# A linear attention with an MLP on one core: the second head of each pair without its swapped copy of v

## The chip, the cores and the metric

One core of a Trainium2 chip runs the whole program. The metric is the time of one execution in device microseconds (us); lower is better. TensorE (PE) multiplies matrices into PSUM, VectorE (DVE), ScalarE (ACT) and GpSimd (POOL) work element by element, and DMA transfers are issued from the queues of SyncE (SP) and of ScalarE.

## What is computed

Four batches of 768 tokens, eight heads of 48 columns. For each head a 48 x 48 state is carried over the tokens, and what it reads out is the x of an MLP with a gate over the tokens:

```python
for t in range(S):
    cur = einsum('bhd,bhe->bhde', u * k_t, v_t)
    y[t] = einsum('bhd,bhde->bhe', r_t, state + cur)
    state = w[:, None] * state + einsum('bhd,bhe->bhde', k_t, v_t)
x = y                                  # (4, 768, 384), heads side by side
u = x + (x^T @ U @ V)^T                # rank 32, over the tokens
out = u + relu(u @ w_ch1) @ w_ch2      # 384 -> 1536 -> 384
```

## The kernel before

**Chunks.** Each batch is six chunks of 128 tokens, and each chunk two halves (i = 0, 1) of 64. The names carry the chunk's number n, from 0 to 23. Within a half, r and k are scaled by powers of w (the tables tabT and tab), so that token-by-token decay becomes a product of matrices: scores = k r^T, masked to earlier tokens (am), times v, plus r times the state at the half's start. The states of successive halves are S; SW is S times w to the power of a half.

**Places on the partitions.** The heads go in pairs q, with j = 0 or 1 in a pair. After a transpose by TensorE (a_tr), head j of a pair has its columns on partitions 64 j to 64 j + 47 of rT and kT. p_sc makes the scores of a half i for head j with the input on half j of the partitions; it writes them to half i for j = 0 and to the *other* half for j = 1 (i ^ j). p_su makes what a half adds to the state. p_out multiplies am with v and rT with S into two PSUM banks pav, one for each row (0, 1: the half of the partitions that is read). Since the scores of j = 1 stand on the other half's partitions, v of the odd heads is loaded a second time with its halves exchanged, as vsw (a_load_odd, two DMAs a chunk). All fp32 products that read one half of the partitions and write one half stand in one of four quarters of the array.

**The steps of a chunk.** a_ks scales k by tab (ks); a_tr transposes r and k and scales them out of PSUM (k by wi, a power of w for each column); a_dv makes r k u, a_dg sums it and multiplies v with the sums, head by head (dv, the token's own term); a_visit(n) is one step of TensorE: the scores and state products of chunk n + 1 first, then the outputs of chunk n; a_am masks the scores, a_st adds up the states and scales them, a_x adds pav of row 0 and of row 1 to dv, which gives x.

**Stages.** The first batch (front(n), n < 6) is worked on alone; filler products ("wake") keep TensorE busy there. Its x goes through c_gx (sums into Gs), then c_xu makes u in two parts (uTh, uTl) and the hidden layer starts: m_1 multiplies u with the first weights, m_2 adds the second product to the output; both weights are loaded and split by VectorE and ScalarE beside it. The chunks of the batches 1 to 3 (18 visits) stand between the products of the MLP of the batch before.

**What sets the order.** Every step is recorded with a due time and a duration in a table of costs, and a planner (class Plan) lays out the order of each engine once, when the program is built. A step that several engines can do goes to the one that the planner expects to be done first. Each engine then runs its order strictly, so a step that waits holds those behind it on its engine.

## Time and profile before

| what | value |
|---|---|
| time, median of 3 runs | 417.44 us (417.15 to 418.97) |
| the profiled execution | 418.57 us, its span 416.9 us |
| PE busy | 401.8 us, 96% |
| DVE busy | 285.4 us, 68% |
| ACT busy | 178.7 us, 43% |
| POOL busy | 63.7 us, 15% |
| DMA | 47.09 MB, 199521 packets |
| granted clock | 0.998 |

The page's busy shares are means over stages of different kinds. The first 50 us are the first batch; up to about 150 us the weights are converted and batch 1 is worked on beside the MLP of batch 0; from there to 340 us follow batches 2 and 3, and then the rest of the last MLP. In the timeline a row has its start, its length, the engine, the line, the operation, output and inputs, and in brackets how long the engine was idle before it and what released it.

### The profile page before, as it was taken

To read this page: it belongs to the slowest core of one execution; us is meant where nothing else is said; L and a number is where in the kernel's file an instruction comes from. 1 tells how busy PE (TensorE), PEld (TensorE's weight loads), DVE (VectorE), ACT (ScalarE), POOL (GpSimd) and SP (SyncE) were. 2 spreads that over 40 slices of the span, in tenths; PEclk is the share of its full clock that TensorE was granted. 3 is DMA by queue.
4 is the path that set the end of the run, shared out by engine and by line. 5 is a ranking of instruction groups with operands and counts; after the bars stand their busy time and mean duration, and the time that the engine had idled before them with its cause. 6 is when DMAs were issued, how large, how long until landed. Compare 5 with 4: busy or idle time off the path is not lost.

```text
span 416.9 us, 12303 instructions
## 1 busy us (share of the span) xinstructions
PE 401.8 (96%) x5112; PEld 387.0 (93%) x5112; DVE 285.4 (68%) x642; ACT 178.7 (43%) x445; POOL 63.7 (15%) x106
## 2 busy tenths in 40 slices
PE   7798899999999999999999999999999999999994
PEld 7798799989999999999999999999999999999994
DVE  7788898899999997787939759788523462113112
ACT  1578478585644464222124433222424442232330
POOL 1462300044240542103000011110000000000000
PEclk9999999999999999999999999999999999999999
DMA  9987879786976777598458765853100420001001
GB/s 136 149 166 199 205 147 216 188 200 126 247 158 105 170 127 173 76 184 163 96 86 162 116 152 80 155 98 76 60 2 2 79 93 0 2 0 60 0 2 62
DMA packets 199521, 47.09 MB, mean 113 GB/s; under 512 B 183073, under 2 KB 197922, under 8 KB 199458
## 3 DMA queue, kind: packets, MB, share of 16 engines
q1 hardware_dynamic: 194274, 44.75, 53.3%
q10 hardware_dynamic: 5184, 1.48, 2.1%
q8 instruction: 42, 0.69, 0.7%
q14 instruction: 21, 0.17, 0.1%
HBM read 37.95 MB, written 8.26 MB: 111 GB/s over the span
## 4 chain that ended last, share of the span: by engine, by line
PE 70%; DVE 12%; DMA 8%; SPq 4%; ACT 3%; issue 2%; ACTq 1%; DVEq 0%
PE p L344 58%; DMA raw_w<-in_moe_w_ch_dram 4%; PE pab L776 2%; SPq L678 2%; PE pav L814 2%; DMA vsw<-in_v_dram 2%; PE pav L820 2%; PE pab L791 2%; DMA ldv<-in_v_dram 2%; DVE raw_w L546 1%; DVE raw_w L543 1%; DVE hl L1108 1%; DVE x L888 1%; PE wake L344 1%; SPq L515 1%
## 5 line engine op out<-in xcount | busy, mean ns | idle before, releaser
L344 PE MATMUL p<-uTh,w1s 128*128 128x384 f32 x576 | 148.1, 338 | 0.2 <-ACT hr L1106 0.2
L1108 DVE TENSOR_TENSOR hl<-hr,hh 128x384 fp32r<-128x384 f32 x90 | 50.7, 564 | 103.9 <-ACT hh L1107 102.4
L1106 ACT ACTIVATE hr<-p 128x384 f32<-128x384 f32 x96 | 47.0, 490 | 169.1 <-PE p L344 164.6
L344 PE MATMUL p<-w2s,hh 128*128 128x384 f32 x576 | 118.9, 338 | 0.0
L344 PEld LDWEIGHTS p<-uTh,w1s 128*128 128x128 f32 x576 | 103.0, 188 | 1.9 <-ACT hr L1106 1.2
L344 PEld LDWEIGHTS p<-w2s,hh 128*128 128x128 f32 x576 | 100.6, 188 | 1.2 <-DVE x L1146 0.3
L344 PE MATMUL p<-uTl,w1s 128*128 128x384 f32 x288 | 96.4, 335 | 0.0
L344 PE MATMUL p<-w2s,hl 128*128 128x384 f32 x288 | 66.4, 335 | 0.5 <-DVE hl L1108 0.5
L344 PEld LDWEIGHTS p<-uTl,w1s 128*128 128x128 f32 x288 | 54.1, 188 | 0.0
L344 PEld LDWEIGHTS p<-w2s,hl 128*128 128x128 f32 x288 | 51.3, 188 | 0.8 <-DVE hl L1108 0.8
L1107 ACT CAST hh<-hr 128x384 fp32r<-128x384 f32 x96 | 49.2, 512 | 2.6
L708 ACT ACTIVATE dv<-ldv,dg 128x48 f32<-128x48 f32 x88 | 21.3, 325 | 4.7 <-DVE dg L704 4.7
L776 PEld LDWEIGHTS pab<-rT,kT 48*64 48x64 f32 x768 | 13.6, 134 | 8.1 <-issue 3.7
L776 PE MATMUL pab<-rT,kT 48*64 48x64 f32 x768 | 17.0, 224 | 2.6 <-DVE rT L747 1.4
L1146 DVE TENSOR_TENSOR x<-p,x 128x384 f32<-128x384 f32 x33 | 16.3, 545 | 3.1 <-PE p L344 3.1
L688 POOL MEMSET ks<- 128x128 f32 x24 | 4.9, 206 | 88.2 <-PE pab L791 86.2
L344 PE MATMUL wake<-ident 128*128 128x128 f32 x114 | 16.4, 299 | 1.7 <-POOL ident masks.py:199 1.7
L881 DVE TENSOR_TENSOR am<-pab,mask 128x256 f32<-128x256 f32 x48 | 17.9, 412 | 0.0
L814 PE MATMUL pav<-vsw,am 64*64 64x48 f32 x384 | 17.1, 220 | 0.1
L814 PE MATMUL pav<-ldv,am 64*64 64x48 f32 x384 | 17.1, 220 | 0.0
L344 PEld LDWEIGHTS wake<-ident 128*128 128x128 f32 x114 | 15.4, 215 | 1.7 <-POOL ident masks.py:199 1.7
L918 POOL TENSOR_TENSOR SW<-S,wm 112x192 f32<-112x192 f32 x24 | 12.2, 508 | 29.0 <-DVE S L909 27.5
(134 smaller groups left out, 506.0 us busy)
## 6 DMA issues: line engine op xcount, KB each, us to landing
raw_w<-in_moe_w_ch_dram SPq DMA_DIRECT2D x24, 384.0 KB, 5.3
ldv<-in_v_dram SPq DMA_DIRECT2D x24, 192.0 KB, 4.3
out_dram<-x SPq DMA_DIRECT2D x21, 192.0 KB, 2.1
ldr<-in_r_dram SPq DMA_DIRECT2D x20, 192.0 KB, 3.8
ldk<-in_k_dram SPq DMA_DIRECT2D x20, 192.0 KB, 3.6
bl<-in_r_dram SPq DMA_DIRECT2D x79, 48.0 KB, 2.5
bl<-in_k_dram SPq DMA_DIRECT2D x79, 48.0 KB, 2.7
ud<-x SPq DMA_DIRECT2D x18, 192.0 KB, 3.1
```

What stands on the lines that cost most here:

```text
L344: return nc.tensor.matmul(*args, **kw)
L678: dma(lambda eng, g=g, s0=s0, ln=ln, sv=sv: eng.dma_start(t.t[32 * g:32 * g + 32, q, :, s0:s0 + ln], sv), [(t, (q, g, s0))], [], 384, 128, ...
L708: nc.scalar.activation(dv.t[:, h], vt()[:, h], AF.Copy, scale=dg.t[:, h:h + 1])
L776: return [lambda q=q, i=i: nc.tensor.matmul(pt.t[(i ^ j) * C2:(i ^ j) * C2 + C2, q * C2:(q + 1) * C2], lhsT=kT.t[rows, q, i * C2:(i + 1) * ...
L791: return nc.tensor.matmul(pt.t[j * HP:j * HP + m, SU + q * D:SU + (q + 1) * D], lhsT=ks.t[half, 2 * q + j, :m], rhs=vt()[half, 2 * q + j, ...
L814: return nc.tensor.matmul(to(q, j, i), lhsT=am[j].t[half, q, :], rhs=vsw[n].t[half, q, :] if j else vt()[half, 2 * q, :], start=(q == 0), ...
L881: on_dve(256, lambda e: e.tensor_tensor(am.t, abs_[n][j].t[:, :SU].rearrange("p (h t) -> p h t", h=NP), mask_.unsqueeze(1).broadcast_to([1 ...
L918: e.tensor_mul(dec.t, new.t, wm.t.broadcast_to([PD, NP, D]))
L1106: on_act(384, lambda: nc.scalar.activation(hr.t, pt.t[:, :TB], AF.Relu), [hr], [pt])
L1107: on_act(384, lambda: nc.scalar.copy(hh.t, hr.t), [hh], [hr])
L1108: on_either(384, lambda e: e.tensor_tensor(hl.t, hr.t, f32(hh.t), ALU.subtract), [hl], [hr, hh])
L1146: on_dve(384, lambda e, x=x, pt=pt: e.tensor_tensor(x.t, pt.t[:, :DM], x.t, ALU.add), [x], [pt])
```

## The change

The scores of j = 1 now stay on their own half (p_sc), so that both heads of a pair take the same v, and vsw with its DMAs is gone. In p_out the 8 value products of a row then read and write that row's half; the state products of that row are four on the same half (together "own", 12) and four on the other ("far"), in the order own, far, own, own. They now take the decayed state SW in place of S, since k's scaling by wi is left out of kT, which becomes a plain copy; tab changes accordingly (its table tw is a copy). Where there is no state yet, the far products take a matrix of zeros (none).

In the first batch alone, a visit becomes two steps (scores and states of chunk n + 1; outputs of chunk n), dv is added by TensorE with the identity (p_dv), a_x is a copy by ScalarE of row 1 and one addition by VectorE, and k from the third chunk on is scaled by GpSimd. In the other batches the two additions of a_x become one step. The copy of tab goes from ScalarE to VectorE. In the planner's table a product of c_gx counts 115 and not 225, the gate products of m_2 now depend on hh, and S and SW have 2 and 4 buffers for 4 and 2.

```diff
...
@@ -451,18 +449,16 @@
         on_dve(4, lambda e: e.tensor_mul(wm.t, top(0), top(0)), [wm], [sq])
 
         tw = xbuf([PD, NP, C], F32, "bl", 5, "tw")
-        on_dve(512, lambda e: e.tensor_mul(subs(tw.t), table(1), wm.t.unsqueeze(2).broadcast_to([PD, NP, 2, C2])), [tw],
-               [wm, tabT], port=True)
+        on_dve(512, lambda e: e.tensor_copy(subs(tw.t), table(1)), [tw], [tabT], port=True)
         on_dve(128, lambda e: e.tensor_mul(tt[:, 0, :, :HC], pw[:, 0], top(1).broadcast_to([PD, NP, HC])), [tabT], [sq])
-        on_dve(4, lambda e: e.tensor_mul(wi.t, top(1), top(1)), [wi], [sq])
         pt = bank("tr", "pt_tab")
 
...
         pe(900, turn, [pt], [tw])
-        on_act(384, lambda: nc.scalar.copy(tab.t.rearrange("p (h d) -> p h d", d=D),
-                                           pt.t.rearrange("p (h d) -> p h d", d=HP)[:, :, :D]), [tab], [pt])
+        on_dve(384, lambda e: e.tensor_copy(tab.t.rearrange("p (h d) -> p h d", d=D),
+                                            pt.t.rearrange("p (h d) -> p h d", d=HP)[:, :, :D]), [tab], [pt])
 
     def flags():
 
...
@@ -645,19 +641,6 @@
             dma(lambda q, i=i, src=src: q.dma_start(part(i)[:, :, :D], src[b, :, c * C:(c + 1) * C, :].rearrange("h p d -> p h d")),
                 [ts[i]] if n < 4 else [(ts[i], "d")], [], 1024, 192, eng=eng)
         rs[n], ks_[n], vs[n] = [((lambda i=i: part(i)), (([(t3, i), (t3, f"pad{i}")] if i < 2 else [tv]) if n < 4 else [(ts[i], "d"), (ts[i], f"pad{i}")])) for i in range(3)]
-        if n < 4 or not front(n):
-            a_load_odd(n)
-
-    def a_load_odd(n, dk=0.0):
-
-        b, c = divmod(n, NCH)
-        t = (xbuf([128, NP, D], F32, "x", NX, f"vsw_{n}") if front(n) else wbuf([128, NP, D], F32, "vsw", 3, f"vsw_{n}"))
-        for i in range(2):
-            s0 = c * C + i * C2
-            dma(lambda q, i=i, s0=s0: q.dma_start(t.t[(1 - i) * C2:(2 - i) * C2],
-                                                  v[b, 1::2, s0:s0 + C2, :].rearrange("h p d -> p h d")),
-                [(t, i)], [], 256, 192, ns=610, eng="ACT" if n < 3 else "SP", dk=dk)
-        vsw[n] = t
 
     bls = {}
 
@@ -687,7 +670,7 @@
         ks = kss[n] = wbuf([128, H, HP], F32, "ks", NK, f"ks_{n}")
         op("POOL", 250, lambda: nc.gpsimd.memset(ks.t[:, :, D:], 0.0), [(ks, "pad")], [])
         on_either(384, lambda e: e.tensor_mul(ks.t[:, :, :D], kt()[:, :, :D], by_head(tab.t)), [(ks, "d")], kb + [tab],
-                  only="DVE" if front(n) else None)
+                  only=("POOL" if n > 1 else "DVE") if front(n) else None)
 
     def a_dv(n):
         (rt, rb), (kt, kb) = rs[n], ks_[n]
@@ -746,18 +729,9 @@
         if i == 0 or n == 0:
             on_dve(512, lambda e: e.tensor_tensor(subs(xT.t[:PD]), subs(by_pair()), table(i), ALU.mult), [xT], [pt, tabT])
             return
-
-
-        def four(q0=0, q1=NP):
-            for q in range(q0, q1):
-                nc.scalar.activation(xT.t[:PD, q], by_pair()[:, q], AF.Copy, scale=wi.t[:, q])
-        if front(n) and n > 1:
-            for q in range(0, NP, 2):
-                op("ACT", 2 * act(C) - 94, lambda q=q: four(q, q + 2), [(xT, q)], [pt, wi])
-            return
-        one_of([("ACT", NP * (act(C) - 94) + 94, four, False),
-                ("DVE", dve(512), lambda: nc.vector.tensor_mul(xT.t[:PD], by_pair(), wi.t.broadcast_to([PD, NP, C])), False)],
-               [xT], [pt, wi])
+        one_of([("ACT", act(512), lambda: nc.scalar.copy(xT.t[:PD], by_pair()), False)]
+               + ([] if front(n) else [("DVE", dve(512), lambda: nc.vector.tensor_copy(xT.t[:PD], by_pair()), False)]),
+               [xT], [pt])
 
 
 
@@ -773,8 +747,8 @@
         rT, kT = trs[n]
         pt = abs_[n][j]
         rows = head_rows(j)
-        return [lambda q=q, i=i: nc.tensor.matmul(
-            pt.t[(i ^ j) * C2:(i ^ j) * C2 + C2, q * C2:(q + 1) * C2], lhsT=kT.t[rows, q, i * C2:(i + 1) * C2],
+        return [lambda q=q, i=i ^ j: nc.tensor.matmul(
+            pt.t[i * C2:(i + 1) * C2, q * C2:(q + 1) * C2], lhsT=kT.t[rows, q, i * C2:(i + 1) * C2],
             rhs=rT.t[rows, q, i * C2:(i + 1) * C2], start=True, stop=True) for q in range(NP) for i in range(2)]
 
     def p_su(n, i):
...
@@ -804,29 +779,38 @@
         vt = vs[n][0]
         rT = trs[n][0]
         pt = pav[row]
+        half = slice(row * C2, (row + 1) * C2)
+        rows = head_rows(row)
+
+        def to(h, i):
+            return pt.t[i * C2:(i + 1) * C2, h * D:(h + 1) * D]
+
+        def av(h):
+            return nc.tensor.matmul(to(h, row), lhsT=am[h % 2].t[half, h // 2, :], rhs=vt()[half, h, :],
+                                    start=(h == 0), stop=False, skip_group_check=True)
+
+        def sq(q, i):
+            rhs = decayed[n, i].t[rows, q, :] if (n, i) in decayed else none.t[rows, :]
+            return nc.tensor.matmul(to(2 * q + row, i), lhsT=rT.t[rows, q, i * C2:(i + 1) * C2], rhs=rhs,
+                                    start=(i != row and q == 0), stop=False, skip_group_check=True)
+
+        def by_state(i):
+            if (n, i) not in decayed and (n == 0 or i == row):
+                return []
+            return [lambda q=q: sq(q, i) for q in range(NP)]
+        own, far = [lambda h=h: av(h) for h in range(H)] + by_state(row), by_state(1 - row)
         ps_ = []
-
-        def to(q, j, i):
-            return pt.t[i * C2:(i + 1) * C2, (2 * q + j) * D:(2 * q + j + 1) * D]
-
-        def av(q, j, i):
-            half = slice(row * C2, (row + 1) * C2)
-            return nc.tensor.matmul(to(q, j, i), lhsT=am[j].t[half, q, :],
-                                    rhs=vsw[n].t[half, q, :] if j else vt()[half, 2 * q, :],
-                                    start=(q == 0), stop=False, skip_group_check=True)
-
-        def sq(q, i):
-            rows = head_rows(row)
-            return nc.tensor.matmul(to(q, row, i), lhsT=rT.t[rows, q, i * C2:(i + 1) * C2], rhs=St[n, i].t[rows, q, :],
-                                    start=False, stop=(q == NP - 1), skip_group_check=True)
-        for q in range(NP):
-            for i in range(2):
-                ps_.append(lambda q=q, i=i: av(q, i ^ row, i))
-        for q in range(NP):
-            for i in range(2):
-                if (n, i) in St:
-                    ps_.append(lambda q=q, i=i: sq(q, i))
+        while own or far:
+            ps_ += own[:1] + far[:1] + own[1:3]
+            own, far = own[3:], far[1:]
         return ps_
+
+    def p_dv(n, row):
+
+        half = slice(row * C2, (row + 1) * C2)
+        return [lambda: nc.tensor.matmul(pav[row].t[half, :DM], lhsT=ident_[half, half],
+                                         rhs=dvs[n].t[half].rearrange("p h d -> p (h d)"), start=False, stop=True,
+                                         skip_group_check=True)]
 
     def in_turn(*lists):
         for k_ in range(max(map(len, lists))):
...
@@ -871,9 +855,16 @@
         def visit():
             in_turn(*other)
             in_turn(*mine)
-        pe(1750 if nxt else 900, visit, wr, rd, tiled=True)
-        if nxt:
-            taken(n + 1)
+        if front(n):
+            if nxt:
+                pe(850, lambda: in_turn(*other), abs_[n + 1], reads(n + 1), tiled=True)
+                taken(n + 1)
+            own = [*ams[n], *vs[n][1], trs[n][0]] + [decayed[n, i] for i in range(2) if (n, i) in decayed]
+            pe(1150, lambda: [in_turn(*mine), in_turn(p_dv(n, 0), p_dv(n, 1))], list(pav), own + [dvs[n]], tiled=True)
+        else:
+            pe(1750 if nxt else 900, visit, wr, rd, tiled=True)
+            if nxt:
+                taken(n + 1)
         a_x(n)
 
     def a_am(n, j):
@@ -884,9 +875,15 @@
     def a_x(n):
         dv = dvs[n]
         x = xs[n] = xbuf([128, DM], F32, "x", NX, f"x_{n}")
-        for row, more in ((0, lambda: dv.t.rearrange("p h d -> p (h d)")), (1, lambda: x.t)):
-            on_dve(384, lambda e, row=row, more=more: e.tensor_tensor(x.t, pav[row].t[:, :DM], more(), ALU.add),
-                   [x], [pav[row], dv])
+
+        def both():
+            nc.vector.tensor_tensor(x.t, pav[0].t[:, :DM], dv.t.rearrange("p h d -> p (h d)"), ALU.add)
+            nc.vector.tensor_tensor(x.t, pav[1].t[:, :DM], x.t, ALU.add)
+        if front(n):
+            on_act(384, lambda: nc.scalar.copy(x.t, pav[1].t[:, :DM]), [x], [pav[1]])
+            on_dve(384, lambda e: e.tensor_tensor(x.t, pav[0].t[:, :DM], x.t, ALU.add), [x], [pav[0]])
+        else:
+            op("DVE", 2 * dve(DM) - 76, both, [x], [*pav, dv])
 
     held = {}
 
...
@@ -910,9 +907,7 @@
                        [new], [pt, decayed[n, j]])
             nk = (n, 1) if j == 0 else (n + 1, 0)
             St[nk] = new
-            if nk[0] % NCH == NCH - 1 and nk[1] or nk[0] % NCH == 0 and nk[1] == 0:
-                continue
-            dec = decayed[nk] = wbuf([PD, NP, D], F32, "SW", 2, f"SW_{nk[0]}_{nk[1]}")
+            dec = decayed[nk] = wbuf([PD, NP, D], F32, "SW", 4, f"SW_{nk[0]}_{nk[1]}")
 
             def one(e, dec=dec, new=new):
                 e.tensor_mul(dec.t, new.t, wm.t.broadcast_to([PD, NP, D]))
...
@@ -1130,7 +1125,7 @@
         if gates:
             for i in range(TPB):
                 pt = ops[b * NCH + t * TPB + i]
-                pe(MM, lambda i=i, pt=pt: gate(i, pt), [pt], [Gs[b], V3])
+                pe(MM, lambda i=i, pt=pt: gate(i, pt), [pt], [Gs[b], V3, hh])
         parts = [(part, m, h, i) for part, m, h in ((high, 2, hh), (low, 1, hl)) for i in range(TPB)]
         if b == B - 1 and t == NTB - 1 and last:
 
...
```

What that makes of the orders is seen in three places.

TensorE's outputs of chunk 13 (the second of batch 2), the rows that follow its next scores. Before:

```order
L814 MATMUL pav0_86<-ldv_13_2566,am_13_0_3012 64x48
L814 MATMUL pav1_98<-vsw_13_2576,am_13_1_3023 64x48
L814 MATMUL pav0_86<-vsw_13_2576,am_13_1_3023 64x48
L814 MATMUL pav1_98<-ldv_13_2566,am_13_0_3012 64x48
L814 MATMUL pav0_86<-ldv_13_2566,am_13_0_3012 64x48
```

And after:

```order
L789 MATMUL pav0_95<-ldv_13_2511,am_13_0_2965 64x48
L789 MATMUL pav1_102<-ldv_13_2511,am_13_0_2965 64x48
L794 MATMUL pav0_95<-SW_13_1_2968,rT_13_2503 64x48
L794 MATMUL pav1_102<-SW_13_0_2834,rT_13_2503 64x48
L789 MATMUL pav0_95<-ldv_13_2511,am_13_1_2975 64x48
L789 MATMUL pav1_102<-ldv_13_2511,am_13_1_2975 64x48
L789 MATMUL pav0_95<-ldv_13_2511,am_13_0_2965 64x48
L789 MATMUL pav1_102<-ldv_13_2511,am_13_0_2965 64x48
```

pav0 is row 0 and pav1 row 1. Before, a row's products alternate between the two halves that they write; after, one in four of them (on SW of the other half) writes the other half.

ScalarE's queue at the start of the program. Before:

```order
L657 DMA vsw_0_91<-in_v_dram 64x4x48 x2
L385 ACT_TABLE_LOAD
L385 COPY outside_76<-ident_67 1x1
L645 DMA ld_0_105<-in_k_dram 128x8x48
L1275 COPY sel_120<-ident_67 128x384
L645 DMA ld_1_109<-in_k_dram 128x8x48
L657 DMA vsw_1_137<-in_v_dram 64x4x48 x2
L645 DMA ld_2_114<-in_k_dram 128x8x48
L657 DMA vsw_2_184<-in_v_dram 64x4x48 x2
L464 COPY tab_206<-pt_tab_195 128x384
```

And after:

```order
L384 ACT_TABLE_LOAD
L384 COPY outside_76<-ident_67 1x1
L1271 COPY sel_91<-ident_67 128x384
L641 DMA ld_0_106<-in_k_dram 128x8x48
L641 DMA ld_1_111<-in_k_dram 128x8x48
L641 DMA ld_2_115<-in_k_dram 128x8x48
L691 ACTIVATE dv_0_171<-ldv_0_127,dg_0_243 128x48 x4
L732 COPY kT_1_274<-ptk_1_247 112x512
```

Three loads of k are all that is left of the DMAs there; the copy of tab is on VectorE, behind rT of chunk 0.

TensorE where the hidden layer starts. Before:

```order
L344 MATMUL wake2_1043<-V3_941 128x512 x4
L344 MATMUL p2_0_0_1072<-Gs_0_1035,V3_941 128x384
L344 MATMUL p2_1_0_1076<-Gs_0_1035,V3_941 128x384
L344 MATMUL p2_2_0_1081<-Gs_0_1035,V3_941 128x384
L344 MATMUL p1_0_0_0_1085<-uTh_0_0_1054,w1s_0_933 128x384 x2
```

And after:

```order
L343 MATMUL wake2_1006<-V3_900 128x512 x4
L343 MATMUL p1_0_0_0_1036<-uTh_0_0_1017,w1s_0_894 128x384 x2
L343 MATMUL p1_0_0_0_1036<-uTl_0_0_1028,w1s_0_894 128x384
L343 MATMUL p1_0_0_0_1036<-uTh_0_0_1017,w1s_0_894 128x384 x2
L343 MATMUL p1_0_0_0_1036<-uTl_0_0_1028,w1s_0_894 128x384
```

p1 are the products of m_1, p2 those of m_2 with the gate products on Gs. Before, the three gate products stand ahead of the first p1; after, they stand behind the second group of p1.

More of the change, by code (lines that the diff above doesn't have):

```diff
@@ L604, in rwkv_moe @@
     NB = B * NCH
-    rs, ks_, vs, vsw = {}, {}, {}, {}
+    rs, ks_, vs = {}, {}, {}
     kss, dvs, dgs = {}, {}, {}
@@ L799, in rwkv_moe @@
     pav = [Buf(ps, [128, 512], F32, None, 1, f"pav{row}") for row in range(2)]
+    none = cbuf([PD, D], F32, "none")
     def p_out(n, row):
@@ L861, in a_visit @@
         nxt = (n + 1) % NCH
-        rd = [*ams[n], vsw[n], *vs[n][1], trs[n][0]] + [St[n, i] for i in range(2) if (n, i) in St]
+        rd = [*ams[n], *vs[n][1], trs[n][0]] + [decayed[n, i] for i in range(2) if (n, i) in decayed]
         wr = list(pav)
@@ L900, in a_st @@
                 continue
-            new = wbuf([PD, NP, D], F32, "S", 4, f"S_{n}_{j}")
+            new = wbuf([PD, NP, D], F32, "S", 2, f"S_{n}_{j}")
             pt = abs_[n][j]
@@ L1269, in rwkv_moe @@
     SOON = 3
+    at(-101, lambda: on_dve(48, lambda e: e.memset(none.t, 0.0), [none], []))
     for p in pav:
```

8 lines of the change are left out of this document (2 added, 6 removed).

## The prediction

> **What bounds the kernel now.** I read the page's busy tenths first (TensorE at 9 from 50 us to the end), then the windows, then the chain of waits from its end backwards.
>
> ```profile
> 40.00:50.00 10.00, 8.32 (x184) 7.51 (x181) 8.96 (x19) 4.13 (x9) 3.47 (x6) 1.00 0.88 216
> 50.00:150.00 100.00, 98.12 (x1254) 91.92 (x1255) 95.37 (x211) 64.25 (x164) 25.45 (x31) 1.00 0.81 171
> ```
>
> The columns of a window are PE, weight load, DVE, ACT and POOL busy time, then the granted clock and the DMA share. From 50 us on TensorE hardly pauses (98.12 of 100), at a granted clock of 1.00. Before 50 us it idles or runs filler, while VectorE is at 8.96 of 10. So two things set the end: when the first hidden-layer products start, and how much work TensorE has after that. The chain of waits in the second half shows that work; its columns are start, length, what:
>
> ```profile
> 153.94 0.62 PE pab L776 x32
> 154.56 0.45 PE pab L791 x27
> ...
> 163.56 0.40 PE pav L820 x14
> ...
> 195.15 0.62 PE pab L776 x32
> ...
> 196.70 0.47 PE pav L820 x30
> 197.16 8.01 PE p L344 x45
> ...
> 216.73 0.61 PE pav L814 x32
> 217.34 0.47 PE pav L820 x32
> ```
>
> Between the p rows stand the visits: scores (L776) and state products (L791) of the next chunk, then the value (L814) and state (L820) products of this one. Each visit delays p by its whole length: 195.15 to 197.16 is 2.01 us, and a chunk's outputs alone, 216.73 to 217.81, are 1.08.
>
> **Part 1, the visits.** A product here works in one quarter of the array, given by the half of the partitions it reads and the half it writes. Each of these fp32 products stands as two records. In the kernel before, the 16 value and 16 state products of a visit (row by row, i by i) put 8 into each quarter, so 16 records. Two comparisons tell what the time goes by. First, scores and states alone put 16 records into the fullest quarter and take 1.08 (153.94 to 155.02), the outputs alone 16 and 1.08, a full visit 32 and 2.01. So 16 further records in a quarter cost 2.01 - 1.08 = 0.93, or 58 ns each. Second, the batch's first visit has state products for the second half only: 16 records in two quarters, eight each. They take 0.40 (14 of the 16 in that row) where 32 records in four quarters, also eight each, take 0.47. Half the work, nearly the same time: the fullest quarter sets it.
>
> After the change the scores stay on their own half, so all 8 value products of an output row read and write the same half: one quarter takes 8 value and 4 state products (24 records), its neighbour 4 (8 records). The fullest quarter gets 8 records more, 8 x 58 ns = 0.465 us per visit. A visit without an earlier state, or without next scores, also goes from 16 to 24 output records in its fullest quarter. There are 18 visits in batches 1 to 3, all where TensorE is full: 18 x 0.465 = **+8.4 us**. Below, the bound is 0 (if something else than the quarter sets it, the first rival); above, 16.7, if the neighbour's products also have to wait their turn in the written order (16 products in a row instead of 8). I take 8.4, because both comparisons give the fullest quarter. The small zero products for chunks without a state go into the emptier quarter: 0.
>
> **Part 2, the start of the first batch.**
>
> ```profile
> 7.55 0.56 DVE L696 TENSOR_TENSOR dv<-ld 128x384 f32<-128x384 f32 x1 [0.60 <-DMA ld<-in_k_dram]
> 9.24 3.17 ACTq L657 DMA_DIRECT2D vsw<-in_v_dram  x2
> 9.83 0.68 DVE L747 TENSOR_TENSOR rT<-ptr,tabT 112x512 f32<-112x512 f32 x1
> 12.45 0.48 ACT L464 COPY tab<-pt_tab 128x384 f32<-128x384 f32 x1 [8.05 <-DMA vsw<-in_v_dram]
> 12.96 1.03 DVE L689 TENSOR_TENSOR ks<-ld,tab 128x384 f32<-128x384 f32 x2 [1.99 <-ACT tab L464]
> 12.98 0.69 PE L776 MATMUL pab<-rT,kT 48*64 48x64 f32 x32 [1.18 <-ACT tab L464]
> ```
>
> The copy of the table sits on ScalarE's queue behind the loads of the swapped v. Those are gone and the copy goes to VectorE, right behind rT: 9.83 + 0.68 + 0.55 = 11.06, and the first k scaling follows there instead of at 12.96: -1.9. The load of the first k was also issued behind two swapped loads, and VectorE waited 0.60 for it: up to -0.6 more. I take **-2.2**; bounds -1.0 (another load late) and -2.5.
>
> **Part 3, the middle chunks of the first batch.**
>
> ```profile
> 22.93 0.69 PE L776 MATMUL pab<-rT,kT 48*64 48x64 f32 x32
> 32.74 0.69 PE L776 MATMUL pab<-rT,kT 48*64 48x64 f32 x32
> L881 DVE TENSOR_TENSOR am<-pab,mask 128x256 f32<-128x256 f32 x12 | 4.6, 415 | 0.0
> L909 DVE TENSOR_TENSOR S<-pab,SW 112x192 f32<-112x192 f32 x10 | 3.5, 351 | 1.7 <-PE pab L791 1.2 <-ACT SW L922 0.5
> L918 DVE TENSOR_TENSOR SW<-S,wm 112x192 f32<-112x192 f32 x3 | 1.4, 459 | 0.0
> L689 DVE TENSOR_TENSOR ks<-ld,tab 128x384 f32<-128x384 f32 x4 | 2.3, 585 | 2.0 <-ACT tab L464 2.0
> L759 DVE TENSOR_TENSOR kT<-ptk,wi 112x512 f32<-112x512 f32 x1 | 0.7, 678 | 0.0
> L708 ACT ACTIVATE dv<-ldv,dg 128x48 f32<-128x48 f32 x48 | 11.8, 328 | 4.2 <-DVE dg L704 4.2
> 41.44 1.57 PE L344 MATMUL pv<-raw_v,sel 128*96 128x192 f32 x8 [0.17 <-DMA ldv<-in_v_dram]
> ```
>
> Two chunks took 9.81, so 4.9 each. After, a chunk's outputs are a step of their own behind its scores, and the next scores stand behind them in TensorE's order. The loop is then: scores and states 1.08; S 0.35, am 0.41, SW 0.46, am 0.41 on VectorE, since the state products now read the decayed state (SW); outputs 1.08 + 0.465; and the new sum of dv by TensorE. That last is two 384-column fp32 products side by side, which no row shows. The nearest, pv, takes 1.57 for eight records of 192 columns, 0.20 each: a record of twice the columns would take 0.40, two of them 0.8 (upper bound); at p's pitch (8.01 / 45 = 0.18 for 384 columns) two take 0.36 (lower). I take 0.6, the middle. Sum 1.08 + 1.63 + 1.55 + 0.6 = 4.9, as now: **0**, with bounds of 0.2 a turn either way. What leaves the engines there (an x addition of 0.55 (42.09 below) per chunk and the later k scalings of 0.585 off VectorE, one kT copy for four activations on ScalarE) lies beside this loop. The added wait is that TensorE now stands for dv, made by eight activations of 0.328 on ScalarE; behind it wait the next scores. Eight of them, 2.6, and two copies of about 0.5 fit into a turn of 4.9.
>
> GpSimd now scales k, four times. Its price is a collision:
>
> ```profile
> 42.09 0.55 DVE L888 TENSOR_TENSOR x<-pav,dv 128x384 f32<-128x384 f32 x1
> 44.13 1.03 POOL L696 TENSOR_TENSOR dv<-ldr,ldk 128x384 f32<-128x384 f32 x1
> 44.64 0.94 DVE L546 SCALAR_TENSOR_TENSOR raw_w<-raw_w 128x384 int32<-128x384 int32 x1
> 45.50 0.55 DVE L543 SCALAR_TENSOR_TENSOR raw_w<-raw_w 128x384 int32<-128x384 int32 x1
> ```
>
> While GpSimd multiplied, a weight step on VectorE took 0.94 against 0.55. Four more GpSimd steps: between 0 and 4 x 1.03; I take one such collision, **+0.4**. The Trainium skill ("SBUF — State Buffer", the single rule on the shared port pair) says that a VectorE instruction with two SBUF inputs and a GpSimd one that reads SBUF exclude each other for a whole instruction; by that, the cost would be near the upper end, and this one row shows a delay of 0.39.
>
> **Part 4, the end of the first batch.**
>
> ```profile
> 37.38 1.91 PE L344 MATMUL wake<-x,Uf 128*96 128x128 f32 x16 [1.09 <-issue]
> 49.23 0.55 DVE L954 TENSOR_TENSOR Gs<-wake,Gs 32x384 fp32r<-32x384 f32 x1
> 52.29 1.37 PE L344 MATMUL p<-Gs,V 96*128 96x384 f32 x3
> 53.50 0.51 PE L344 MATMUL p<-uTh,w1s 128*128 128x384 f32 x2
> ```
>
> Today it is 16.5 from the fifth chunk's scores (32.74) to the end of the sums (Gs, 49.23). After: one turn 4.9, last scores 0.85, pv 1.57 and seven x sums 1.7 (two records each, 0.12 a record, by the row at 37.38), outputs and dv 2.15, eight x sums 1.9, nine transposes 1.1, three x sums 0.7, the two copies into Gs 0.75 (an estimate: the 0.55 of the row at 49.23 and the start of a shorter one before it): 15.6, so **-0.9**, bounds +1.0 and -3.0. Then three gate products stand ahead of the first hidden-layer products and hold TensorE from 52.29 to 53.50, though three need 3 x 0.18 = 0.53; they now come after the first two groups, when nothing holds them: 1.21 - 0.53, some **-0.8** with the first group's earlier start (0 to -1.2).
>
> **Part 5, weights.**
>
> ```profile
> 71.56 0.36 DVE L536 TENSOR_SCALAR raw_w<-raw_w 128x384 int32<-128x384 uint8 x1 [1.57 <-DMA raw_w<-in_moe_w_ch_dram]
> 72.44 0.62 PE L344 MATMUL p<-w2s,hl 128*128 128x384 f32 x2 [0.49 <-DVE hl L1108]
> ```
>
> VectorE waited 1.57 for a weight from SP's queue, the step behind (hl) came late, and TensorE stood for it at 72.44. Twelve swapped loads that SP issues before that weight are gone, at a time when its queue is one issue behind the other: this wait goes, **-0.6** (0 to -1.5).
>
> **Sum**: 8.4 - 2.2 + 0 + 0.4 - 0.9 - 0.8 - 0.6 = +4.3. The profiled execution took 418.57 (span 416.9 and 1.7 around it), so 422.9; it lies 1.1 above the median of 417.44, so **421.7** is what I predict for the median.
>
> **Rivals.** (1) *The half, not the quarter.* If products that read the same half wait for each other, a visit has 16 output products per half before and after, and costs nothing more: 421.7 - 8.4 = **413.3**. For it: nothing but that all full visits are balanced by half too. Against it: the 0.40 row, which should then be near 0.24. The Trainium skill ("TensorE: Matmul & The Clock Gate", Part 3, the mechanism) states that a weight load overlaps running products only where the row group differs, which is this rival; the row of 0.40 disagrees.
> (2) *The first batch is bound by VectorE's sum.* Then it shortens by what leaves VectorE: six additions 3.3, four scalings 2.3, a kT 0.7 and the idle 2.0, less four more SW 1.8 and the table 0.55, so 6.0 instead of 2.7 (parts 2 to 4 without the gates); 8.4 - 6.0 - 0.8 - 0.6 = +1.0: **418.4**, no change. For it: VectorE is 8.96 of 10 busy, and 95.37 of 100 up to 150 us. Against: the loop of part 3, and TensorE's 98.12 beside that.
> (3) *The split costs.* The transposes of a chunk on TensorE (eight of 0.13 by the row below, 1.0 a chunk) now lie between scores and outputs, and dv may come late; if they aren't covered by the 1.63 of VectorE, four turns grow by 1.0 each: **425.7**.
>
> ```profile
> 43.50 1.04 PE L344 MATMUL pu<-ident,x 128*128 128x128 f32 x8
> ```
>
> That the swapped copy's loads are hidden anyway would take away parts 2 and 5 (to 424.5), inside the range.
>
> **Numbers.** Forecast 0.51 (own range 419 to 424), (1) 0.10, (2) 0.25, (3) 0.14. Leaving out (1) and about half of (3): 416.5 to 426.0. A change of less than 0.5%, 2.1 us, can't be told from none: faster is below 415.4, nearly only (1), 0.12; within, 0.29, most of (2) and the low tail of the forecast; slower 0.59.
>
> **What would show it.** Full visits in the second half of 2.47 instead of 2.01 and outputs alone of 1.55 prove part 1; 2.01 makes (1) right. The first scores near 10.8, the table on VectorE behind rT; the fifth chunk's scores near 30.5; Gs near 46.5, the first p<-uTh near 50; no wait near 69 to 72. A first p<-uTh before 46 makes (2) right, one after 53 (3). I am wrong in the total if visits don't lengthen, or if the first batch gains more than twice what I say.

## The result, and the profile after

| | before | after |
|---|---|---|
| median of four runs each, us | 417.41 | 424.20 (423.65 to 425.2) |
| ratio | | 1.0157, 95% interval 1.0126 to 1.0189 |
| profiled execution, us | 418.57 | 425.20 |
| its span, us | 416.9 | 423.3 |
| first scores of the first batch | 12.98 | 11.00 |
| scores of its second, third, fourth, fifth, last chunk | 17.44, 22.93, 27.75, 32.74, 39.21 | 15.15, 21.71, 26.63, 32.64, 38.23 |
| Gs on VectorE | 49.23 | 49.24 |
| first products with the second weights (w2s) | 57.60 | 57.35 |
| first scores of the third batch | 153.94 | 154.57 |

The change made the kernel slower by 6.8 us. First the visits, in the chain of waits of the changed kernel (start, length, what):

```profile
197.09 0.62 PE pab L750 x32
...
199.55 8.01 PE p L343 x45
...
219.59 0.19 PE pav L789 x2
...
221.12 8.01 PE p L343 x45
```

A full visit now delays p from 197.09 to 199.55, by 2.46 (2.01 before), and outputs alone take 219.59 to 221.12, 1.53 (1.08 before). That is 0.45 for each of 18 visits, 8.1 in all. So everything else together gained only 1.3 (8.1 - 6.8). Where it did not gain is seen in the first batch; this is TensorE's timeline there, with the idle time before an instruction and what ended it in brackets:

```profile
11.00 0.69 PE L750 MATMUL pab<-rT,kT 48*64 48x64 f32 x32
15.15 0.69 PE L750 MATMUL pab<-rT,kT 48*64 48x64 f32 x32 [0.34 <-DVE rT L730]
21.71 0.33 PE L750 MATMUL pab<-rT,kT 48*64 48x64 f32 x4
26.63 0.33 PE L750 MATMUL pab<-rT,kT 48*64 48x64 f32 x4
31.90 0.25 PE L789 MATMUL pav<-ldv,am 64*64 64x48 f32 x1 [0.39 <-issue]
32.64 0.33 PE L750 MATMUL pab<-rT,kT 48*64 48x64 f32 x4
37.13 0.26 PE L789 MATMUL pav<-ldv,am 64*64 64x48 f32 x2 [0.81 <-issue]
49.85 0.50 PE L343 MATMUL wake<-V 96*128 96x512 f32 x1 [0.49 <-DVE Gs L949]
52.30 0.59 PE L343 MATMUL p<-uTh,w1s 128*128 128x384 f32 x2
54.63 0.55 PE L343 MATMUL pu<-ident,x 128*128 128x128 f32 x3 [0.52 <-DVE uTl L1032]
```

The first scores come 1.98 earlier than before. Three turns later, at the fifth chunk's scores (32.64), the lead is 0.10: from the second chunk's scores to there it takes 17.49 instead of 15.30. Gs is not earlier at all. Two of TensorE's pauses are ended by "issue": the engine waited for nothing that the profile shows. The windows after answer those quoted of before:

```profile
40.00:50.00 10.00, 9.51 (x128) 8.46 (x128) 7.73 (x15) 5.48 (x13) 4.28 (x7) 1.00 0.45 75
50.00:150.00 100.00, 98.32 (x1258) 93.79 (x1259) 95.67 (x210) 65.47 (x165) 27.44 (x30) 1.00 0.76 161
```

VectorE is freer than before from 40 to 50 us (7.73 of 10 instead of 8.96) and not from there to 150 (95.67 of 100).

### The profile page after: what moved, and what is told of

It is laid out like the page before. It is cut to its first block, busy times and chain, and to the rows that moved or that the text cites. A ratio compares the mean times of both kernels' runs of the same rounds, so it can differ in the third digit from the quotient of the medians.

```text
span 423.3 us, 12252 instructions
## 1 busy us (share of the span) xinstructions
PE 411.5 (97%) x5130; PEld 396.4 (94%) x5130; DVE 283.8 (67%) x635; ACT 182.2 (43%) x448; POOL 70.0 (17%) x105
## 3 DMA queue, kind: packets, MB, share of 16 engines
q10 hardware_dynamic: 3552, 1.18, 1.1%
## 4 chain that ended last, share of the span: by engine, by line
PE 93%; DVE 4%; ACT 1%; issue 1%; POOL 0%; DVEq 0%; POOLq 0%
PE p L343 71%; PE pav L789 5%; PE pav L794 4%; PE pab L750 3%; PE wake L343 3%; PE pab L765 2%; PE ptk L721 1%; PE pav L811 1%; PE ptr L721 1%; PE pu L343 1%; PE pG L959 1%; DVE x L1141 1%; DVE uTl L1032 0%; ACT dv L691 0%; PE ph L343 0%
## 5 line engine op out<-in xcount | busy, mean ns | idle before, releaser
L1103 DVE TENSOR_TENSOR hl<-hr,hh 128x384 fp32r<-128x384 f32 x91 | 52.4, 575 | 104.9 <-ACT hh L1102 99.3
L794 PE MATMUL pav<-SW,rT 48*64 48x48 f32 x704 | 37.3, 226 | 0.0
L789 PE MATMUL pav<-ldv,am 64*64 64x48 f32 x768 | 28.6, 219 | 1.2 <-issue 1.2
L789 PEld LDWEIGHTS pav<-ldv,am 64*64 64x64 f32 x768 | 25.8, 134 | 3.1 <-issue 2.1
L794 PEld LDWEIGHTS pav<-SW,rT 48*64 48x64 f32 x704 | 28.6, 132 | 0.0
L750 PEld LDWEIGHTS pab<-rT,kT 48*64 48x64 f32 x768 | 14.8, 134 | 6.1 <-issue 5.1
L750 PE MATMUL pab<-rT,kT 48*64 48x64 f32 x768 | 17.9, 224 | 0.3 <-DVE rT L730 0.3
L906 DVE TENSOR_TENSOR S<-pab,SW 112x192 f32<-112x192 f32 x40 | 13.9, 347 | 5.7 <-PE pab L765 5.7
```

The source lines that it names most:

```text
L750: return [lambda q=q, i=i ^ j: nc.tensor.matmul(pt.t[i * C2:(i + 1) * C2, q * C2:(q + 1) * C2], lhsT=kT.t[rows, q, i * C2:(i + 1) * C2], r ...
L789: return nc.tensor.matmul(to(h, row), lhsT=am[h % 2].t[half, h // 2, :], rhs=vt()[half, h, :], start=(h == 0), stop=False, skip_group_chec ...
L794: return nc.tensor.matmul(to(2 * q + row, i), lhsT=rT.t[rows, q, i * C2:(i + 1) * C2], rhs=rhs, start=(i != row and q == 0), stop=False, s ...
L906: on_dve(192, lambda e, new=new, ptv=ptv, dec=decayed[n, j]: e.tensor_tensor(new.t, ptv(), dec.t, ALU.add), [new], [pt, decayed[n, j]])
L1103: on_either(384, lambda e: e.tensor_tensor(hl.t, hr.t, f32(hh.t), ALU.subtract), [hl], [hr, hh])
```

## The experiments

Three groups of kernels ran. Where a text says "the changed kernel's 424.2", that is the median above; the kernel before had medians of 417.78, 417.27 and 417.31 beside the three groups.

### Is it the fullest quarter?

**Swapped copy back in batches 1 to 3** (the first batch stays as changed):

```
-  lambda q, i=i ^ j: matmul(pt[i*C2:(i+1)*C2, ...], kT, rT)
+  lambda q, i=i: matmul(pt[(i^j)*C2:(i^j)*C2+C2, ...], kT, rT)     # n >= NCH
+  av(q, j, i): rhs = vsw[n] if j else v, for both halves i          # n >= NCH
+  if not front(n): a_load_odd(n)
```

> The changed kernel, but batches 1 to 3 again place odd heads' scores on the other half, load the swapped copy of v and spread a row's value products over both halves; the first batch stays as changed. Theory of the fullest quarter: full visits go back from 2.46 to 2.01 and outputs alone from 1.54 to 1.08, 18 x 0.45 = 8.1 less than the changed kernel's 424.2, so 416.1; a little more if the twelve loads per batch make weights late again (one wait of 0.6 near 72). Rival, that visits are longer since state products now read another tensor or alternate with value products, whatever their quarter: visits stay near 2.46 and the time at 424. On the first batch it says: everything before 50 us as in the changed kernel, first p<-uTh within 0.3 of it.

In this kernel, and in the last of the third group, the parts of the two output banks that no product writes in batches 1 to 3 keep the sums of the first batch's last chunk, and x has them added; clearing each bank once, off TensorE, between 50 and 83 us would be the remedy.

Measured: 419.44, ratio to before 1.0042 (1.0018 to 1.0066).

**Far state products left out**, and **four value products left out**, in batches 1 to 3:

```
-  own, far = [av(h) for h in range(H)] + by_state(row), by_state(1 - row)
+  own, far = [av(h) for h in range(H)] + by_state(row), by_state(1 - row) if front(n) else []
```

```
-  own, far = [av(h) for h in range(H)] + by_state(row), by_state(1 - row)
+  own, far = [av(h) for h in range(H if front(n) else NP)] + by_state(row), by_state(1 - row)
```

> The changed kernel, with the four state products of each output row that write the other half left out in batches 1 to 3 (that part of the output is left out). They are the ones in the emptier quarter. Theory of the fullest quarter: nothing to gain, a full visit stays at 2.46, the time at 424.2 (within 1). Rival, the number of products in the written order or per half read: 16 of 64 records of the outputs less, a quarter of 1.54 per visit, 18 x 0.38 = 6.9 less, so 417.3.

> The changed kernel, with four of the eight value products of each output row left out in batches 1 to 3 (the last four heads' own values are left out). As many products as in the run without the far state products, but from the fullest quarter: 16 records there instead of 24. Theory of the fullest quarter: full visit 2.00, outputs alone 1.08, 424.2 - 8.1 = 416.1. Rival, number of products: the same as for the run without the far state products, 417.3 if that one is 417.3.

Measured: 425.04 (1.0171, 1.0109 to 1.0232) without the far products, 417.39 (0.9997, 0.9976 to 1.0017) without the four value products. The chain of waits without the far state products:

```profile
197.59 0.62 PE pab L750 x32
...
200.05 8.01 PE p L343 x45
...
220.08 1.06 PE pav L789 x32
221.61 8.01 PE p L343 x45
```

and without the four value products:

```profile
192.74 0.62 PE pab L750 x32
...
194.73 8.01 PE p L343 x45
...
214.30 0.19 PE pav L789 x2
...
215.36 8.01 PE p L343 x45
```

Eight products a visit are left out in both, so 16 records. Out of the emptier quarters they save nothing: 200.05 - 197.59 = 2.46 and 221.61 - 220.08 = 1.53, to the hundredth the changed kernel's. Out of the fullest quarters they save 0.47 (1.99 and 1.06). So neither the number of products, nor how many read one half, nor the far products' place among the others sets a visit; the fullest quarter does. That value products cost more than state products can't be the reason for the longer visits either, since a full visit has 16 of each before and after. Part 1's mechanism is shown, and so is its size.

The swapped copy's return shows the same (a full visit from 195.02 to 197.03):

```profile
195.02 0.62 PE pab L761 x32
...
197.03 3.34 PE p L343 x18
```

But its time is 419.4 and not the 416.1 expected. Four waits that the changed kernel hasn't or has shorter stand in its timeline, three of them in these rows:

```profile
103.14 0.62 PE L343 MATMUL p<-uTh,w1s 128*128 128x384 f32 x2 [0.98 <-ACT hr L1119]
230.50 0.59 PE L343 MATMUL pu<-V,Gs 96*128 96x384 f32 x2 [0.36 <-DVE Gs L991]
232.06 0.44 PE L343 MATMUL pu<-V,Gs 96*128 96x384 f32 x1 [0.27 <-DVE xT L1044]
```

They are 1.6 here; the fourth is around 145 us, where TensorE stands 1.95 and in the changed kernel 1.01, so 0.9 longer. That is 2.5 of the 3.3 that are missing; the rest is not followed up. The run without four value products, which loads no swapped copy, has the first of them too (1.03 at 101.91). So visits that are shorter by 8.1 let TensorE run into work of VectorE and ScalarE, and a part is given back.

### What sets the first batch?

**No filler** between scores and outputs of chunks 1 to 5 (13 filler products fewer):

```
-  self.woken.append((x, filler))
+  if x < 14000 or end is not the first batch's: self.woken.append((x, filler))
```

> The changed kernel without the 13 filler products that TensorE runs between scores and outputs of the first batch's chunks 1 to 5 (about 0.25 each, 3.25 in all); fillers before the first scores stay. Theory 1 (as predicted: VectorE's steps between scores and outputs set the turn): TensorE waits instead, Gs stays at 49.2, the time at 424.2. Theory 2 (fillers and transposes, written into gaps that are shorter on the chip, lie on the path): the fifth chunk's scores (33.2 now) come 1.5 to 3 earlier, Gs near 47, the time 421.2 to 422.7. The granted clock should stay at 1.00 there, and if it falls below, the turns get longer and the time is over 424.

Measured: 424.58 (1.0171, 1.0117 to 1.0225), as theory 1 has it. In its profile the fifth chunk's scores come at 31.70, 0.94 earlier, and Gs 1.38; 0.56 of that is shorter pauses ended by "issue" (0.64 for 1.20), and the median shows nothing of it. (The run without four value products has the changed kernel's first batch, and its Gs came 1.56 earlier, so a difference of this size can be chance.) What the fillers covered can be seen now, on TensorE:

```profile
20.03 0.26 PE L791 MATMUL pav<-ldv,am 64*64 64x48 f32 x2 [0.36 <-DVE x L886]
30.26 0.26 PE L791 MATMUL pav<-ldv,am 64*64 64x48 f32 x2 [1.34 <-DVE x L886]
```

and on VectorE, in the same run:

```profile
28.18 0.36 DVE L908 TENSOR_TENSOR S<-pab,SW 112x192 f32<-112x192 f32 x1 [0.80 <-PE pab L767]
...
29.39 0.35 DVE L908 TENSOR_TENSOR S<-pab,SW 112x192 f32<-112x192 f32 x1
29.65 0.55 DVE L886 TENSOR_TENSOR x<-pav,x 128x384 f32<-128x384 f32 x1
```

The outputs of a chunk wait for the x addition of the chunk before (there is one pair of output banks), and that addition stands on VectorE behind S, am, SW, am and the next S: from 28.18 to 30.20, 2.0 and not the 1.63 that the prediction gave VectorE's part of the loop. The prediction's loop has no x addition in it.

**One-step visits, dv added by VectorE** (undoes the split and the sum on TensorE in the first batch), and **two steps, dv added by VectorE** (undoes the sum alone):

```
-  if front(n): scores step; outputs step with p_dv        # one step: the branch is gone
-  on_act(copy x <- pav[1]); on_dve(x <- pav[0] + x)
+  on_dve(x <- pav[0] + dv); on_dve(x <- pav[1] + x)
```

> The changed kernel with the first batch's visits in one step again and its x summed by VectorE out of both banks and dv, as before the change; k stays scaled on GpSimd from the third chunk on. The visits of all batches keep the longer quarter. Theory 1 (moving dv's sum from VectorE to TensorE exchanges 0.55 on one engine for 0.65 on the other, both in one loop of scores, VectorE's steps, outputs): no difference, 424.2 +- 1. Theory 2 (the split and the sum on TensorE cost): the five turns get 0.65 to 1.0 shorter, Gs 3 earlier, 421. Theory 3 (the split is a gain that something else ate): 426.

> The changed kernel with visits in two steps as changed, but dv added by VectorE instead of by two 384-column products on TensorE and a copy on ScalarE. TensorE loses 6 x 0.65 = 3.9 of work in the first batch, VectorE gets 6 x 0.55 = 3.3 more. Theory 1 (outputs wait for the x addition of the chunk before, which stands in the loop on VectorE anyway): a turn changes by 0.55 - 0.65 = -0.1, nothing seen, 424.2. Theory 2 (TensorE sets the turn): 0.65 a turn less, 420.5 to 421.5.

Measured: 423.81 (1.0141, 1.0101 to 1.018) and 423.3 (1.0131, 1.009 to 1.0173): neither can be told from the changed kernel. For the one-step kernel that is theory 1. For the other the time says theory 1 and the turns say theory 2: its scores come at 11.43, 15.56, 20.22, 24.32 and 29.17, so the fifth chunk's are 3.5 earlier than in the changed kernel. Then comes this, on TensorE, and in its windows:

```profile
35.21 0.24 PE L794 MATMUL pav<-SW,rT 48*64 48x48 f32 x1 [2.01 <-issue]
```

```profile
30.00:35.00 5.00, 3.21 (x78) 2.86 (x69) 4.65 (x13) 3.96 (x10) 1.39 (x3) 1.00 1.03 198
35.00:40.00 5.00, 4.79 (x83) 4.70 (x83) 2.28 (x7) 2.79 (x11) 0.51 (x1) 0.51 1.18 258
40.00:45.00 5.00, 5.00 (x86) 4.76 (x86) 1.73 (x5) 0.54 (x1) 2.92 (x5) 0.80 0.14 22
```

A pause of 2.01 with no waiter, and after it a granted clock of 0.51 and 0.80 over ten us: 5 x 0.49 + 5 x 0.20 = 3.45 of TensorE's time. Gs is at 48.65, 0.6 earlier than in the changed kernel, where 3.5 had been in hand. This holds for the profiled execution (424.08). Over the other three, the mean granted clock was 0.993, 0.997 and 0.998, and 3.45 of 422 would be 0.008; at least the last two did not lose so much to the clock, and they took 422.25 and 424.15 all the same. What took the lead there is not shown.

**The early start alone**, as changes of the kernel before: the table copied by VectorE, and the same with the gate products behind.

```
-  on_act(384, lambda: nc.scalar.copy(tab, pt_tab))
+  on_dve(384, lambda e: e.tensor_copy(tab, pt_tab))
```

```
-  pe(MM, gate, [pt], [Gs[b], V3])
+  pe(MM, gate, [pt], [Gs[b], V3, hh])                      # second kernel only
```

> The kernel before with one line changed: the table is copied out of its bank by VectorE instead of ScalarE (where it stands behind the loads of the swapped v). Theory 1, as predicted for the start: first scores at 11.0 instead of 12.98, and the 1.9 is still there at Gs (47.3 instead of 49.2) and at the end: 417.6 - 1.9 = 415.7. Theory 2, the first batch gives the start back whatever the visits look like (pauses of TensorE between 30 and 40 us, the loads' own times): Gs within 0.5 of 49.2, the time at 417.5.

> The kernel before with the table copied by VectorE and the three gate products of the first block put behind the first hidden-layer groups, as the change does. Theory of the prediction: another 0.8 less than with the table alone, so 414.9. Rival: the hidden-layer groups then stand for the next thing that is late (the transposed low parts, uTl, which came at 51.7 before and after the change), and the gain is below 0.3: 415.5.

Measured: 416.92 (0.9988, 0.9969 to 1.0007) with the table alone: the first scores at 11.80, Gs at 48.96, so 1.2 gained at the start, 0.3 left at Gs, and no difference that the runs can tell. Theory 2. The longest of three pauses of TensorE there (the others are 0.59 and 0.57):

```profile
41.31 0.26 PE L820 MATMUL pav<-S,rT 48*64 48x48 f32 x2 [1.18 <-issue]
```

With the gates moved too: 421.56 (1.0105, 1.006 to 1.0149), 4.6 more. No theory had that. The pause after the same instruction is 1.87 there, and the clock falls as above:

```profile
41.83 0.34 PE L820 MATMUL pav<-S,rT 48*64 48x48 f32 x2 [1.87 <-issue]
```

```profile
40.00:45.00 5.00, 3.17 (x12) 2.74 (x12) 4.16 (x11) 2.04 (x4) 2.12 (x4) 0.63 0.92 252
45.00:50.00 5.00, 5.00 (x86) 4.61 (x86) 2.77 (x6) 1.03 (x2) 1.32 (x3) 0.69 0.94 201
```

5 x 0.37 + 5 x 0.31 = 3.4, and Gs comes at 52.35 instead of 48.96. But this explains the profiled execution alone (421.86, mean granted clock 0.989): the other three had 0.995, 0.997 and 0.995, which leaves no room for 3.4, and took 421.00, 423.34 and 421.25. So the cause of the 4.6 is open, and so is what moving the gates is worth by itself.

### What are the pauses?

A new theory was needed for the pauses ended by "issue". Where in TensorE's program they stand gives it. Counting the records of TensorE and its sequencer (matmuls, weight loads, semaphore steps) from the start up to each pause:

| kernel | pause begins, us (length) | instructions before it | less 256 x k |
|---|---|---|---|
| before | 36.28 (1.09) | 1473 | 193 |
| after | 31.51 (0.39), 36.32 (0.81) | 1217, 1473 | 193, 193 |
| far products left out | 31.72 (0.37), 36.52 (1.08) | 1217, 1473 | 193, 193 |
| no filler | 35.63 (0.64) | 1473 | 193 |
| table by VectorE | 17.66 (0.59), 35.48 (0.57), 40.13 (1.18) | 449, 1473, 1729 | 193, 193, 193 |
| table and gates | 17.49 (0.87), 39.96 (1.87) | 449, 1729 | 193, 193 |
| one step | 36.35 (1.11) | 1473 | 193 |
| two steps, dv by VectorE | 33.21 (2.01) | 1473 | 193 |

The kernels differ in what these instructions are; the count is the same, every 256. The page of the changed kernel lists a queue for instructions:

```profile
q8 instruction: 42, 0.69, 0.7%
```

42 packets in 0.69 MB are 16 KB each. In the trace one such packet is moved between each of these points and the next, and its end is what the next point waits for: in the kernel with the pause of 2.01, TensorE passes the point before at 28.93, the packet is on its way from 32.28 to 33.72, and TensorE, at the next point since 33.21, goes on at 35.21. In all the pauses above TensorE goes on 1.25 to 1.65 after its packet's end. The Trainium skill ("Runtime: NRT & Kernel Launch", section "Instruction fetch mechanics") says that an engine's instructions are refilled in 16 KiB blocks of 256 by its own DMA queue, and that passing a block's border is mostly hidden. The block size agrees with 256 here; that it is hidden doesn't, in the first batch: 256 instructions of small products pass in 4.0 to 5.2 us (28.93 from 24.92 in that kernel; in the changed one the pause at 31.51 begins 5.2 after the point at 26.35).

So theory 1 of the last group: the packet stands behind the data that SP loads at that time (weights, the second batch's chunks), and the faster TensorE gets through a block, the longer it stands at the border. The edit holds back the loads that the first batch doesn't need:

```
+  last_am: the instruction that masks the last chunk's first scores (VectorE)
+  add_manual_dep(load, last_am)    # weight blocks 4 to 6, r, k, v (and swapped v) of the second
+                                   # batch's first chunks, its first blocks
+  at(... if i < 5 else max(33 + 0.01 * i, as before), load)    # later weight blocks planned no sooner than 33
```

> The changed kernel with dv added by VectorE (as the run before), and with the loads that the first batch doesn't need held back: SP waits for the last chunk's masked scores before it issues the fourth to sixth weight block, the second batch's first two chunks and its first blocks. Theory 1 (TensorE's pauses without a waiter in the first batch, each after 193 + 256 x k of its instructions, are waits for its next 16 KB of instructions, which stand behind these loads): the pause of 2.01 at 33.2 falls below 0.8, the granted clock stays at 1.00 from 35 to 45 (0.76 and 0.80 without), Gs comes at 46 instead of 48.65, the time is 423.3 - 2.5 = 420.8. Theory 2 (the pauses have nothing to do with transfers): same pause, 423.3; or more, if the held weights come late behind 50 us.

> The changed kernel with those loads held back and nothing else. Theory 1: the pauses of 0.39 and 0.81 at 31.5 and 36.3 go, 424.2 - 1.0 = 423.2; the turns keep dv's sum on TensorE (4.9 to 5.5 each), so no more than that. Theory 2: 424.2.

> The kernel before with the table copied by VectorE, and those loads (with the swapped copies of the second batch's first chunks) held back. Theory 1: the pauses of 0.57 and 1.18 at 35.5 and 40.1 shrink to 0 and under 0.6, the one of 0.59 at 17.7 stays (the loads there are needed), so the early start comes through to Gs at about 47.5: 416.9 - 1.2 = 415.7. Theory 2: 416.9.

> All that paid, in one kernel: the changed kernel with the swapped copy of v and both halves again in batches 1 to 3 (quarters even, full visit 2.01), the first batch in two steps with dv added by VectorE, and the loads held back. By the fullest quarter 18 x 0.45 = 8.1 less than the run with loads held back and the long quarter: 420.8 - 8.1 = 412.7; the swapped loads may make weights late again, which took 1.5 in the first such run, so 412.5 to 414.5, 3 to 5 below the kernel before. If the pauses stay, 415.2.

Measured: 425.17 (1.0173, 1.0128 to 1.0218), 426.86 (1.0208, 1.0157 to 1.0258), 420.24 (1.007, 1.0041 to 1.0099) and 418.38 (1.0008, 0.9974 to 1.0042), all longer than expected. What theory 1 says of the pause at 33 came true with dv on VectorE, in this kernel and again in the last one:

```profile
30.00:35.00 5.00, 5.00 (x193) 4.83 (x190) 4.87 (x14) 3.45 (x8) 0.92 (x3) 1.00 0.03 7
35.00:40.00 5.00, 5.00 (x99) 4.71 (x95) 3.42 (x10) 3.43 (x12) 1.42 (x2) 1.00 0.55 175
```

```profile
43.80 0.55 DVE L972 TENSOR_TENSOR Gs<-wake,Gs 32x384 fp32r<-32x384 f32 x1
```

The DMA share from 30 to 35 is 0.03 (1.03 without the hold), TensorE is busy throughout, the clock stays at 1.00 (without the hold it was 0.51 from 35 to 40, not the 0.76 of the expectation), and Gs comes at 43.80 instead of 48.65. A pause of 0.94 at 28.7 is left, at a border that passed without one when nothing was held. In the changed kernel with the loads held back both pauses are gone and Gs is at 47.42 (49.24). That proves less: the run without four value products, with the same first batch and nothing held, passed both borders without a pause at DMA shares of 0.92 and 1.14 (30 to 35, 35 to 40), since its packets came early enough (ended at 29.74 and 34.25, 1.6 and 1.2 before their borders). And the profiled execution with the hold has a granted clock of 0.91 from 50 to 55 and 0.75 from 55 to 60, 1.7 of TensorE's time, behind two waits for uTl (0.76 and 0.83). In the kernel with the table by VectorE the pause at 35 is 1.95 instead of 0.57: there the packet started only at 34.69, 2.9 after the point before it, in a window with a DMA share of 0.64 from 30 to 35; the hold did not clear the way. The clock did not fall behind this pause:

```profile
37.08 2.10 PE L344 MATMUL wake<-x,Uf 128*96 128x128 f32 x17 [1.95 <-issue]
```

```profile
35.00:40.00 5.00, 3.05 (x69) 2.77 (x68) 3.24 (x9) 3.50 (x11) 0.58 (x2) 1.00 0.34 121
```

But with dv on VectorE the 4.85 gained at Gs is gone by the third batch: its first scores come at 153.5, and at 153.1 without the hold. TensorE's larger waits between:

```profile
49.51 0.61 PE L343 MATMUL p<-uTh,w1s 128*128 128x384 f32 x2 [0.58 <-ACT hr L1124]
88.72 0.59 PE L343 MATMUL p<-w2s,hh 128*128 128x384 f32 x2 [1.06 <-DVE x L1164]
130.36 1.14 PE L343 MATMUL p<-w2s,hh 128*128 128x384 f32 x5 [0.29 <-DVE w2s L569]
137.37 0.44 PE L343 MATMUL p<-w2s,hh 128*128 128x384 f32 x1 [0.65 <-ACT w2s L568]
139.08 1.14 PE L343 MATMUL p<-w2s,hh 128*128 128x384 f32 x5 [1.27 <-DVE w2s L569]
```

They are 3.85, where the kernel without the hold has 0.74 and 0.26. Between Gs and these scores TensorE idles 5.04 in all, and 1.58 without the hold: 3.5 of the 5.3 lost there (109.73 for 104.41) are waits, and the rest is longer busy time, whose cause is open. TensorE stands for weights that VectorE and ScalarE are still splitting, and for x; VectorE is busy 48.59 of the 50 us from 100 to 150. Whether the weights are late because their loads were held, or because VectorE's sum up to 150 us allows no more, these runs don't separate. In the kernel before with the table by VectorE the hold cost 3.3 in the median while Gs moved by 0.17 the wrong way, so the hold alone seems to have a price. Its size is uncertain: the profiled executions differ by 0.8 (418.22 and 417.40), and of the ten runs with the hold (418.19 to 422.89) three had a granted clock of 0.989 to 0.991.

The last kernel takes all that paid: quarters even in batches 1 to 3, dv on VectorE, loads held back. Gs at 43.32, and 418.38 in the end: no difference from the kernel before. It waits 0.93 at 77.55 (kT), 0.80 at 89.18 (x), and 1.74, 0.33 and 0.36 between 130 and 137 (w2s). No version was found that is measurably faster than the kernel before.

## Why the prediction was right, and where it was not

The forecast was 421.7, slower, between 416.5 and 426.0; it is 424.2, slower, just above the forecast's own range of 419 to 424. By its own steps, in the profiled executions (425.20 - 418.57 = +6.6 against +4.3):

| step | predicted | measured |
|---|---|---|
| 1, visits | +8.4 | +8.1 (18 x 0.45) |
| 2, start | -2.2 | -1.98 at the first scores, -2.29 at the second chunk's |
| 3, middle chunks | 0 (0.2 a turn either way) | +2.2 (17.49 for 15.30), 0.39 of it a pause |
| 4, end of the first batch | -0.9 | +0.1 (Gs 16.60 after the fifth chunk's scores, 16.49 before) |
| 4, gates behind | -0.8 | -0.26 (Gs to the first w2s products, 8.11 for 8.37) |
| 5, weights | -0.6 | -1.8 (57.35 to 154.57, less six visits) |
| later, outside the span | 0 | +0.6 |

The signs named came for part 1 (2.46 and 1.53), the start (11.00) and the wait near 72, and not for the rest: the fifth chunk's scores came at 32.64 (30.5 was said), Gs at 49.24 (46.5), the first p<-uTh at 52.30 (50).

- **The visits** were right in mechanism and size. Rival (1), the half, is out: visits did lengthen, and products left out of the emptier quarter save nothing. The Trainium skill's rule that stood beside it in the prediction ("TensorE: Matmul & The Clock Gate", Part 3, the mechanism: a weight load overlaps running products only where the row group differs) has no run here on its side.
- **The start** was right to 0.2, and worth nothing, which the prediction did not see. The failed step is part 3: "0, with bounds of 0.2 a turn". Its loop left out the x addition (0.55), which outputs must wait for because there is one pair of banks; VectorE's part is 2.0, not 1.63. It also took one turn of 4.9 for all, and the turn from 15.15 to 21.71 holds the outputs of two chunks (6.56, before 5.49). And it knew nothing of the instruction blocks, 0.39 of the turn from 26.63 to 32.64 and 0.81 of the next.
- **The sum of dv on TensorE** was sized at 0.6; with it on VectorE the turns are 4.66, 4.10 and 4.85 where the changed kernel has 6.56 (with two chunks' outputs, of which that run has one before), 4.92 and 6.01. So it sat on the loop, as said, and cost 0.8 to 1.2 a turn (with a pause of 0.39 in the last, and of 0.20 in the other run's), more than the 0.6. Little of it came out in the time (423.3); in the profiled execution the block border took 2.01 and the clock 3.45.
- **The collision** on VectorE (+0.4) was put down to the wrong step of GpSimd. Beside the four scalings of k that it now does (13.53, 17.54, 23.74 and 29.39) only an SW at 18.43 is longer, 0.44 for 0.35: 0.1. The two steps that are much longer, a scaling of k of 0.82 for 0.55 at 10.73 and an SW of 0.77 for 0.35 at 17.03, stand beside GpSimd's products for dv, which it has in the kernel before too; the second lies within step 3.
- **The end**: 15.6 was said and 16.6 measured; the pause of 0.81 fell there, and the gates' gain went to the wait of 0.52 for uTl at 54.63.
- **The weights**: the wait named went (0.49 at 72.44), and one that wasn't named (0.54 at 84.94), so more than was said; the one near 147 grew from 0.41 to 1.01.
- Rival (2), VectorE's sum, is wrong as it was put: VectorE got freer before 50 us and Gs did not move. From 50 to 150 us it may be nearly right: with the loads held back, what TensorE gained earlier it met again in part as weights not yet split. Rival (3) has a time (425.7) that is nearer than the forecast's, for another reason: the fillers and transposes between scores and outputs were covered, by VectorE's x.

So the sign and most of the size came from the one term that lies where TensorE is full. The gains were argued one by one from waits that were really there, and three of four did not reach the end. That the total is off by no more than 2.5 is in part luck: the weights gave 1.2 more than was said, in part by a wait that wasn't named.

## What to carry to other kernels

Count small products by the quarter of the array that they read and write, and put the same number into each: a visit here cost about 57 ns more for each further record of its fullest quarter (0.45 to 0.47 for 8), and nothing for the others. Where many small products follow each other, count instructions as well as time: a border every 256 instructions can be a wait with no waiter in the profile, and it shows as the same position in the program at whatever time. A start that comes earlier is a gain only if each stage behind it has slack; look first at the stage where another engine is above 95% busy, and expect that it may take the gain back.
